# The experts' second product in matmuls of 256 columns instead of 512

## The chip, the cores and the metric

The kernel runs on one core of one Trainium2 chip. The metric is the device time of one execution in microseconds (us). Three runs of the kernel before took 2106.46, 2108.26 and 2109.92 us; their median, 2108.26 us, is the time before.

## The reference

A feature attention makes x (2304 tokens, 512 features), a gated product with three matrices makes a new x from it, and eight experts work on that. What the change touches is the last part:

```python
def _moe2_ref(x, w_gate, w1, w2):
    ...
    out = np.zeros((N, D), dtype=np.float32)
    for e in range(E):
        h = np.maximum(x @ w1[e], 0.0)
        ye = h @ w2[e]
        out += P[:, e:e + 1] * ye
    return out.astype(np.float32)
```

Here N = 2304 tokens, D = 512, E = 8 experts, and h has 1024 columns. P is made from x @ w_gate by an exponential and eight rounds of row and column scaling (the Sinkhorn steps).

## The kernel before

Three parts follow each other: the attention (to some 230 us), the gated product (to some 575 us), and the experts. All large products are made from operands that are split in two, a high part of type fp32r and a low part, so one product of tiles is three matmuls (`mm3`, lines 86 to 89): high times high, high times low, low times high. The first operand is the stationary one and is loaded before each matmul; the second is streamed, and its columns are the columns of the matmul.

The experts run in three token stages (`s`) of 768 tokens. In each stage the loop over `units` goes through experts `e` and, within an expert, through four units `p` (`NP` = 4). A unit (lines 724 to 752) makes seven products of 384 columns, 42 matmuls, into tiles `pa` and `ps` of PSUM; VectorE adds them up in `c` (line 741), and `h_split` (lines 720 to 722) makes two h tiles from that: ScalarE's ReLU gives `hH[p]` and `hH[p + 4]`, and VectorE then gives the low parts `hL[p]` and `hL[p + 4]`. So the last unit of an expert makes hH3, hL3, hH7 and hL7. In the first token stage ScalarE, VectorE and GpSimd also split the experts' weights (`prep_w1`, `split_w2`), and at a stage's last expert they split the x of the next stage (`prep_x`).

After an expert's fourth unit comes the second product, `h @ w2[e]`: for six blocks of 128 tokens (`tt`) one bank of PSUM, `py` (128 partitions x 512 columns, two buffers), is filled by eight h tiles in the order 0, 4, 1, 5, 2, 6, 3, 7 (`fts`), three matmuls of 512 columns each:

```python
for n, ft in enumerate(fts):
    hi, lo = W2[ft // 2]
    mm3(ps, hH[ft][:, tcs], hL[ft][:, tcs], hi[:, ft % 2], lo[:, ft % 2], n == 0, n == FT2 - 1)
    if n % 2:
        between()
```

That is 24 matmuls in a bank, 144 for an expert, and 3456 in the program. `between()` calls the next Sinkhorn step as long as there are any (the first expert of the first stage); their matmuls are at line 785 (`cs`). A full bank is read once by VectorE (line 847 or 849), which scales it by P and adds it to `o`.

The order of the instructions on each engine is made when the program is built, by a scheduler that may move an instruction of a later block ahead of one that waits. On the chip each engine goes through its own order, and waits on semaphores of the others.

Another place that the text speaks of is line 165 in the first part: fp32 matmuls of 128 columns, each on 64 of the 128 rows of the array, one for each half (`b`) side by side. The trace has two records for each of them.

Of the kernel before, what the change touches and what calls it, by code (L numbers as in the profile page):

```python
# [27 lines left out]
def kernel(  # L28
# [21 lines left out]
    NT, DM = out.shape  # L50
# [12 lines left out]
    FT2 = DF2 // P  # L63
# [22 lines left out]
    def mm3(ps, aH, aL, bH, bL, start, stop):  # L86
        nc.tensor.matmul(ps, aH, bH, start=start, stop=False)  # L87
        nc.tensor.matmul(ps, aH, bL, start=False, stop=False)  # L88
        nc.tensor.matmul(ps, aL, bH, start=False, stop=stop)  # L89
# [360 lines left out]
    def load_x(s):  # L450
        rawX[s] = rx.tile([P, KT, 2 * N1], F32, name=f"rx{s}", tag="rx")
        nc.sync.dma_start(rawX[s], XS[s])
# [29 lines left out]
    def load_w1(u):  # L482
        if u < len(units):
            s, e, p = units[u]
            if s > 0:
                return
            rawW1[u] = rw1.tile([P, 7, 2 * P], F32, name=f"r1_{u}", tag="r")
            nc.sync.dma_start(rawW1[u][:, 0:3], moe2_w1[e, p][:, 1:4])
            nc.sync.dma_start(rawW1[u][:, 3:7], W1T[u])

    def prep_w1(u):
        if u >= len(units):
            return
        n = u % len(W1S)
        if u >= len(W1S):
            pool = wc1c[0] if u % 3 == 2 else wc1
            hl = pool.tile([P, 2, 7, 2 * P], F32R, name=f"w1_{u}", tag="hl")
            nc.sync.dma_start(f32(hl), W1S[n])
            WC[u] = hl[:, 0], hl[:, 1]
            return  # L500
        r = rawW1.pop(u)
        hl = wc1.tile([P, 2, 7, 2 * P], F32R, name=f"w1_{u}", tag="hl")
        hi, lo = hl[:, 0], hl[:, 1]
        for i, c in enumerate((slice(0, 3), slice(3, 7))):
            copy("Wh", hi[:, c], r[:, c], 2 * u + i)
            subtract("Wl", lo[:, c], r[:, c], f32(hi[:, c]), 2 * u + i)
        nc.sync.dma_start(W1S[n], f32(hl))
        WC[u] = hi, lo

    def sbuf(c, name, bufs=1, side="right"):  # L510
        return c.enter_context(tc.tile_pool(name=name, bufs=bufs, side=side, reuse_waits="tile"))
# [30 lines left out]
    with ExitStack() as c2:  # L542
# [76 lines left out]
        for j in range(NT // N1):  # L619
            c0 = j * N1  # L620
            for ft in range(FT):
                ab = []
                for w in range(2):
                    n = 2 * ft + w
# [7 lines left out]
                    ps = ab_p.tile([P, N1], F32, name=f"ab{j}_{ft}_{w}", tag="ab")  # L632
                    hi, lo = w12[n]
# [25 lines left out]
            for dt in range(KT):  # L659
                ps = px_p.tile([P, N1], F32, name=f"px{j}_{dt}", tag="px")  # L660
                dc = slice(dt * P, (dt + 1) * P)
                for ft in range(FT):
                    hi, lo = w34[ft]
# [25 lines left out]
    with c4:  # L689
# [8 lines left out]
        W2, rawW2 = {}, {}  # L698
        hH = [hp.tile([P, 2 * N1], F32R, name=f"hH{i}") for i in range(FT2)]
        hL = [hp.tile([P, 2 * N1], F32R, name=f"hL{i}") for i in range(FT2)]  # L700

        def load_w2(u):
            if u < len(units):
                s, e, p = units[u]
                t = st.tile([P, 2, DM], F32, name=f"r2_{u}", tag="r")
                nc.sync.dma_start(
                    t, moe2_w2[e, 2 * p * P : 2 * (p + 1) * P, :].rearrange("(j p) d -> p j d", p=P)
                )
                rawW2[u] = t

        def split_w2(u):
            s, e, p = units[u]
            t = rawW2.pop(u)
            hi = wp.tile([P, 2, DM], F32R, name=f"w2h{u}", tag=f"h{p}")
            lo = wp.tile([P, 2, DM], F32R, name=f"w2l{u}", tag=f"l{p}")
            copy("W2h", hi, t, u)
            subtract("W2l", lo, t, f32(hi), u)
            W2[p] = hi, lo
# [5 lines left out]
        def unit(u, between):  # L724
            s, e, p = units[u]
            c = ut.tile([P, 4, N1], F32, name=f"c{u}", tag="c")
            c11, c21, c12, c22 = (c[:, i] for i in range(4))
            B11, B21, B22, T1, T2, T3, T4 = range(7)

            def product(x, i, *adds):  # L730
                ps = ph_p.tile([P, N1], F32, name=f"p{x}{u}", tag="ph")
                (wh, wl), (xh, xl) = WC[u], XC[x]
                for kt in range(2):
                    k = slice(kt * P, (kt + 1) * P)
                    mm3(ps, wh[:, i, k], wl[:, i, k], xh[:, kt], xl[:, kt], kt == 0, kt == 1)
                with tc.high_priority(60):
                    for o, t in adds:
                        if t is None:
                            nc.scalar.copy(o, ps)
                        else:  # L740
                            nc.vector.tensor_tensor(o, t, ps, ALU.add)  # L741
                between()

            product("a11", B11, (c11, None))
            product("s2", T2, (c12, c11))
            product("s3", T3, (c21, c12))
            product("s1", T1, (c22, c21), (c12, c12))
            product("a12", B21, (c11, c11))
            product("a22", T4, (c21, c21))
            h_split(p, c[:, 0:2].rearrange("p a n -> p (a n)"))  # L750
            product("s4", B22, (c12, c12))
            h_split(p + NP, c[:, 2:4].rearrange("p a n -> p (a n)"))
# [47 lines left out]
        def between():  # L800
            if todo:
                todo.pop()()
# [3 lines left out]
        for u, (s, e, p) in enumerate(units):  # L806

            if u + 1 < len(W1S):
                prep_w1(u + 1)
                load_w1(u + 2)  # L810
            if u + 2 == len(W1S):
                c6.close()
                wc1c.append(sbuf(c6, "wc1c", 1, "left"))
            if u + 2 >= len(W1S):
                prep_w1(u + 2)
            unit(u, between)
            split_w2(u)
            load_w2(u + 2)
            if p < NP - 1:
                continue  # L820
            if e == 0 and s + 1 < NSC:
                load_x(s + 1)
            if e == NE - 1 and s + 1 < NSC:
                prep_x(s + 1)
            for tt in range(2 * N1 // P):
                t = s * 2 * N1 // P + tt
                ps = py_p.tile([P, DM], F32, name=f"py{e}_{t}", tag="py")
                tcs = slice(tt * P, (tt + 1) * P)
                if e == 0:
                    oacc[tt] = op.tile([P, DM], F32, name=f"o{t}", tag=f"o{tt}")  # L830
                o = oacc[tt]
                fts = [f for p_ in range(NP) for f in (p_, p_ + NP)]
                for n, ft in enumerate(fts):
                    hi, lo = W2[ft // 2]
                    mm3(ps, hH[ft][:, tcs], hL[ft][:, tcs], hi[:, ft % 2], lo[:, ft % 2], n == 0, n == FT2 - 1)
                    if n % 2:
                        between()
                if todo:
                    pend.append(t)
                    nc.scalar.copy(o, ps)  # L840
                    continue
                for t_ in pend:
                    o_ = oacc[t_]
                    nc.vector.tensor_scalar(o_, o_, Pw[:, t_, 0:1], None, ALU.mult)
                pend = []
                if e == 0:
                    nc.vector.tensor_scalar(o, ps, Pw[:, t, 0:1], None, ALU.mult)  # L847
                else:
                    nc.vector.scalar_tensor_tensor(o, ps, Pw[:, t, e : e + 1], o, ALU.mult, ALU.add)  # L849
                if e == NE - 1:  # L850
                    nc.sync.dma_start(out[t * P : (t + 1) * P, :], o)
# [76 lines left out]
```

## Time and profile before

| | us |
|---|---|
| median of 3 runs (lowest, highest) | 2108.26 (2106.46, 2109.92) |
| the profiled execution | 2110.07 |
| its span, first to last instruction | 2108.3 |
| TensorE (PE) busy in the span | 2050.1 |
| weight loads (PEld) | 1817.4 |
| VectorE (DVE) | 1129.7 |
| ScalarE (ACT) | 597.6 |
| GpSimd (POOL) | 363.0 |

The profile is of one execution. Busy time of an engine is the time in which at least one of its instructions is under way; TensorE's weight loads have a row of their own, since they run beside its matmuls. Matmuls overlap each other, and their ends are modelled, so the rate of TensorE is read from the starts. The releaser of an idle stretch is the instruction that ended the wait. The granted clock is the share of TensorE's full clock in a stretch.

### The profile page before, as it was taken

To read this page: it belongs to the slowest core of one execution; us is meant where nothing else is said; L and a number is where in the kernel's file an instruction comes from. 1 tells how busy PE (TensorE), PEld (TensorE's weight loads), DVE (VectorE), ACT (ScalarE), POOL (GpSimd) and SP (SyncE) were. 2 spreads that over 40 slices of the span, in tenths; PEclk is the share of its full clock that TensorE was granted. 3 is DMA by queue.
4 is the path that set the end of the run, shared out by engine and by line. 5 is a ranking of instruction groups with operands and counts; after the bars stand their busy time and mean duration, and the time that the engine had idled before them with its cause. 6 is when DMAs were issued, how large, how long until landed. Compare 5 with 4: busy or idle time off the path is not lost.

```text
span 2108.3 us, 28910 instructions
## 1 busy us (share of the span) xinstructions
PE 2050.1 (97%) x11877; PEld 1817.4 (86%) x11877; DVE 1129.7 (54%) x1718; ACT 597.6 (28%) x979; POOL 363.0 (17%) x268
## 2 busy tenths in 40 slices
PE   7999899999899999999999999999999999999999
PEld 5667689999788888888888999888999888999887
DVE  7765853333486545665454555434565444555443
ACT  6765532222333222333221222111132111122111
POOL 3433331211322211222220000000010000000000
PEclk9999999999899999999999999999999999999999
DMA  6432445555565555655564444334454334444330
GB/s 216 144 118 84 137 134 155 185 155 155 198 247 182 192 196 220 249 198 192 185 230 150 180 180 149 134 107 151 179 190 179 131 107 153 170 180 174 124 117 30
DMA packets 78531, 345.44 MB, mean 164 GB/s; under 512 B 7488, under 2 KB 11456, under 8 KB 65728
## 3 DMA queue, kind: packets, MB, share of 16 engines
q1 hardware_dynamic: 77808, 342.95, 45.6%
q8 instruction: 93, 1.52, 0.3%
q10 hardware_dynamic: 592, 0.66, 0.1%
q14 instruction: 38, 0.31, 0.0%
HBM read 256.54 MB, written 87.03 MB: 163 GB/s over the span
## 4 chain that ended last, share of the span: by engine, by line
PE 82%; DVE 6%; ACT 3%; DMA 3%; issue 3%; POOL 3%; SPq 0%; ACTq 0%; POOLq 0%; DVEq 0%
PE py L89 13%; PE py L88 12%; PE py L87 12%; PE ps L87 5%; PE ps L89 5%; PE ps L88 5%; PE pa L87 4%; PE pa L89 4%; PE pa L88 4%; PE ab L89 3%; PE ab L87 3%; PE ab L88 3%; PE px L88 1%; PE px L89 1%; PE px L87 1%
## 5 line engine op out<-in xcount | busy, mean ns | idle before, releaser
L89 PE MATMUL py<-w2h,hL 128*128 128x512 f32 x1152 | 457.1, 397 | 0.2
L87 PE MATMUL py<-w2h,hH 128*128 128x512 f32 x1152 | 456.8, 397 | 0.4 <-DVE o L847 0.4
L88 PE MATMUL py<-w2l,hH 128*128 128x512 f32 x1152 | 456.9, 397 | 0.0
L849 DVE SCALAR_TENSOR_TENSOR o<-py,Pw,o 128x512 f32<-128x512 f32 x126 | 94.6, 750 | 451.5 <-PE py L89 451.4
L99 POOL TENSOR_TENSOR w2l<-r,w2h 128x1024 fp32r<-128x1024 f32 x48 | 116.4, 2424 | 1109.2 <-ACT w2h L96 1100.2
L741 DVE TENSOR_TENSOR c<-c,ps 128x384 f32<-128x384 f32 x480 | 255.7, 548 | 88.8 <-PE ps L89 83.1
L96 ACT CAST w2h<-r 128x1024 fp32r<-128x1024 f32 x96 | 101.0, 1052 | 695.2 <-PE py L89 612.7
L89 PEld LDWEIGHTS py<-w2h,hL 128*128 128x128 f32 x1152 | 216.8, 188 | 55.3 <-DVE hL L722 3.0
L87 PEld LDWEIGHTS py<-w2h,hH 128*128 128x128 f32 x1152 | 217.0, 188 | 52.5 <-DVE o L847 0.8
L88 PEld LDWEIGHTS py<-w2l,hH 128*128 128x128 f32 x1152 | 217.0, 188 | 51.5
L722 DVE SCALAR_TENSOR_TENSOR hL<-c,hH 128x768 fp32r<-128x768 f32 x192 | 233.0, 1230 | 28.0 <-ACT hH L721 26.4
L721 ACT ACTIVATE hH<-c 128x768 fp32r<-128x768 f32 x192 | 158.0, 843 | 298.7 <-DVE c L741 276.7
L87 PE MATMUL ab<-XH,wH 128*128 128x384 f32 x384 | 131.2, 342 | 8.6 <-DVE wH L96 8.6
L89 PE MATMUL ab<-XH,wL 128*128 128x384 f32 x384 | 131.6, 343 | 1.1 <-DVE wL L99 1.1
L88 PE MATMUL ab<-XL,wH 128*128 128x384 f32 x384 | 130.9, 341 | 0.0
L741 DVE TENSOR_TENSOR c<-c,pa 128x384 f32<-128x384 f32 x192 | 102.2, 548 | 16.7 <-PE pa L89 15.2
L643 POOL TENSOR_TENSOR cL<-a,cH 128x384 fp32r<-128x384 f32 x48 | 58.8, 1227 | 235.1 <-ACT cH L642 235.0
L99 POOL TENSOR_TENSOR w<-r,w 128x768 fp32r<-128x768 f32 x32 | 66.6, 2081 | 129.6 <-ACT w L96 124.8
L99 DVE TENSOR_TENSOR w2l<-r,w2h 128x1024 fp32r<-128x1024 f32 x48 | 59.0, 1229 | 54.7 <-ACT w2h L96 54.7
L96 ACT CAST w<-r 128x768 fp32r<-128x768 f32 x64 | 59.6, 938 | 97.8 <-DMA r<-in_moe_w_dram 31.0
L641 DVE TENSOR_TENSOR a<-ab,a 128x384 f32<-128x384 f32 x48 | 26.7, 556 | 108.6 <-PE ab L89 108.6
L87 PEld LDWEIGHTS ab<-XH,wH 128*128 128x128 f32 x384 | 72.9, 190 | 10.4 <-DVE wH L96 8.3
(174 smaller groups left out, 3840.8 us busy)
## 6 DMA issues: line engine op xcount, KB each, us to landing
w<-w1s SPq DMA_DIRECT2D x64, 1792.0 KB, 7.6
w1s<-w SPq DMA_DIRECT2D x32, 1792.0 KB, 6.6
r<-in_moe_w_dram SPq DMA_DIRECT2D x96, 512.0 KB, 3.5
rw<-in_w_dram SPq DMA_DIRECT2D x32, 512.0 KB, 3.8
tr<-in_moe_w_dram SPq DMA_DIRECT2D x32, 512.0 KB, 4.3
w1t<-tt SPq DMA_DIRECT2D x32, 512.0 KB, 5.1
r<-w1t SPq DMA_DIRECT2D x32, 512.0 KB, 8.1
r<-in_moe_w_dram SPq DMA_DIRECT2D x32, 384.0 KB, 7.5
```

Of the source, the lines that this page charges most:

```text
L87: nc.tensor.matmul(ps, aH, bH, start=start, stop=False)
L88: nc.tensor.matmul(ps, aH, bL, start=False, stop=False)
L89: nc.tensor.matmul(ps, aL, bH, start=False, stop=stop)
L96: (e.copy if e is nc.scalar else e.tensor_copy)(out, src)
L99: engine(key, i).tensor_tensor(out, a, b, ALU.subtract)
L641: behind = nc.vector.tensor_tensor(cc, ab[1], a_sb, ALU.mult).ins
L643: nc.gpsimd.tensor_tensor(l, cc, f32(h), ALU.subtract)
L721: nc.scalar.activation(hH[ft], src, AF.Relu)
L722: nc.vector.scalar_tensor_tensor(hL[ft], src, 0.0, f32(hH[ft]), ALU.max, ALU.subtract)
L741: nc.vector.tensor_tensor(o, t, ps, ALU.add)
L849: nc.vector.scalar_tensor_tensor(o, ps, Pw[:, t, e : e + 1], o, ALU.mult, ALU.add)
```

## The change

Each bank is filled in two halves (`hf`) of 256 columns, one after the other. For each half all eight h tiles are gone through, so every h tile is the stationary operand twice as often. The bank, the instruction that reads it and the number of calls of `between()` in a bank (four) are the same.

```diff
-                for n, ft in enumerate(fts):
-                    hi, lo = W2[ft // 2]
-                    mm3(ps, hH[ft][:, tcs], hL[ft][:, tcs], hi[:, ft % 2], lo[:, ft % 2], n == 0, n == FT2 - 1)
-                    if n % 2:
-                        between()
+                for hf in range(2):
+                    dc = slice(hf * DM // 2, (hf + 1) * DM // 2)
+                    for n, ft in enumerate(fts):
+                        hi, lo = W2[ft // 2]
+                        mm3(
+                            ps[:, dc], hH[ft][:, tcs], hL[ft][:, tcs],
+                            hi[:, ft % 2, dc], lo[:, ft % 2, dc], n == 0, n == FT2 - 1,
+                        )
+                        if n % 4 == 3:
+                            between()
```

All 3456 matmuls of `py` with 512 columns become 6912 with 256. On TensorE, the end of the first pass through the h tiles in the first bank of expert 2, first token stage, stood so before (`py2_0` is the bank of expert 2, block 0; the last operand is the stationary one):

```order
L87 MATMUL py2_0_7238<-w2h11_7232,hH6_5846 128x512
L88 MATMUL py2_0_7238<-w2l11_7233,hH6_5846 128x512
L89 MATMUL py2_0_7238<-w2h11_7232,hL6_5854 128x512
L87 MATMUL py2_0_7238<-w2h9_7078,hH3_5843 128x512
L88 MATMUL py2_0_7238<-w2l9_7079,hH3_5843 128x512
L89 MATMUL py2_0_7238<-w2h9_7078,hL3_5851 128x512
L87 MATMUL py2_0_7238<-w2h11_7232,hH7_5847 128x512
L88 MATMUL py2_0_7238<-w2l11_7233,hH7_5847 128x512
L89 MATMUL py2_0_7238<-w2h11_7232,hL7_5855 128x512
```

The last of these is matmul 24 of the bank, with 23 ahead of it. In the changed kernel the same place, in the first half of the bank, reads:

```order
L87 MATMUL py2_0_7526<-w2h9_7366,hH3_5843 128x256
L88 MATMUL py2_0_7526<-w2l9_7367,hH3_5843 128x256
L89 MATMUL py2_0_7526<-w2h9_7366,hL3_5851 128x256
L87 MATMUL py2_0_7526<-w2h11_7520,hH7_5847 128x256
L88 MATMUL py2_0_7526<-w2l11_7521,hH7_5847 128x256
L87 MATMUL py2_1_7576<-w2h8_7289,hH0_5840 128x256
L88 MATMUL py2_1_7576<-w2l8_7290,hH0_5840 128x256
L89 MATMUL py2_1_7576<-w2h8_7289,hL0_5848 128x256
L87 MATMUL py2_1_7576<-w2h10_7443,hH4_5844 128x256
L89 MATMUL py2_0_7526<-w2h11_7520,hL7_5855 128x256
L87 MATMUL py2_0_7526<-w2h8_7289,hH0_5840 128x256
```

Four matmuls of the next bank (`py2_1`) have moved ahead of the one with hL7, which has 27 matmuls ahead of it now; the second half of the bank follows. It is so for experts 2 to 6 of this stage; for expert 1 there are 30 ahead, for expert 7 there are 34, and for expert 7 of the second stage 35. At the 15 other experts after the first no matmul is moved, and 23 are ahead.

On ScalarE, at the last unit of expert 2 in the first stage (unit 11, whose sums are in `c11`; `w1` is the weight of later units), the order before was:

```order
L739 COPY c11_7170<-pa1111_7171 128x384
L721 ACTIVATE hH6_5846<-c10_7093 128x768
L96 CAST w1_12_7161<-r1_12_7090 128x1024
L96 CAST w1_13_7394<-r1_13_7167 128x768
L721 ACTIVATE hH3_5843<-c11_7170 128x768
L721 ACTIVATE hH7_5847<-c11_7170 128x768
L96 CAST w1_13_7394<-r1_13_7167 128x1024
```

and is now:

```order
L739 COPY c11_7458<-pa1111_7459 128x384
L721 ACTIVATE hH6_5846<-c10_7381 128x768
L96 CAST w1_12_7449<-r1_12_7378 128x1024
L721 ACTIVATE hH3_5843<-c11_7458 128x768
L721 ACTIVATE hH7_5847<-c11_7458 128x768
L96 CAST w1_13_7826<-r1_13_7455 128x768
L96 CAST w1_13_7826<-r1_13_7455 128x1024
```

The cast of `w1_13` with 768 columns has moved from before hH3 to behind hH7. VectorE's order at these places is as before.

## Rows read from the trace of the kernel before

**Rows 1.** The page: busy time of each engine, and the chain by engine.
```profile
PE 2050.1 (97%) x11877; PEld 1817.4 (86%) x11877; DVE 1129.7 (54%) x1718; ACT 597.6 (28%) x979; POOL 363.0 (17%) x268
...
PE 82%; DVE 6%; ACT 3%; DMA 3%; issue 3%; POOL 3%; SPq 0%; ACTq 0%; POOLq 0%; DVEq 0%
```

**Rows 2.** The page's costliest groups: busy us, mean ns of one, idle before.
```profile
L88 PE MATMUL py<-w2l,hH 128*128 128x512 f32 x1152 | 456.9, 397 | 0.0
...
L88 PEld LDWEIGHTS py<-w2l,hH 128*128 128x128 f32 x1152 | 217.0, 188 | 51.5
```

**Rows 3.** Window of second stage: us, busy PE, PEld, DVE, ACT, POOL (count), clock, DMA.
```profile
1127.00:1614.00 487.00, 487.00 (x2405) 434.03 (x2405) 234.76 (x338) 99.52 (x129) 42.76 (x18) 1.00 0.40 148
```

**Rows 4.** Timeline of TensorE, expert 1 of second stage: start us, us, instruction.
```profile
1190.06 0.39 PE L87 MATMUL py<-w2h,hH 128*128 128x512 f32 x1
...
1223.79 0.34 PE L87 MATMUL pa<-a11h,w 128*128 128x384 f32 x1
...
1252.94 0.39 PE L87 MATMUL py<-w2h,hH 128*128 128x512 f32 x1
```

**Rows 5.** Timeline at the start of a second product: matmuls and a load.
```profile
1000.83 0.40 PE L88 MATMUL py<-w2l,hH 128*128 128x512 f32 x1
1000.83 0.19 PEld L89 LDWEIGHTS py<-w2h,hL 128*128 128x128 f32 x1
...
1001.06 0.39 PE L89 MATMUL py<-w2h,hL 128*128 128x512 f32 x1
```

**Rows 6.** Timeline of lines 605 and 606 (six matmuls), and their loads' group.
```profile
300.50 0.34 PE L605 MATMUL lg<-XH,WG 128*16 128x384 f32 x1
...
301.37 0.34 PE L606 MATMUL lg<-XL,WG 128*16 128x384 f32 x1
...
L606 PEld LDWEIGHTS lg<-XL,WG 128*16 128x16 f32 x24 | 2.3, 94 | 5.0 <-DVE XL L671 3.7
```

**Rows 7.** Timeline of line 165, and tile pp: ns min/median/max of its records.
```profile
103.31 0.72 PE L165 MATMUL pp<-wpr,k 64*128 64x128 f32 x9
...
L165 PEld LDWEIGHTS pp<-wpr,k x288: 182/188/330, 3.5 to 216.6; 64*128 64x128 f32 x144
L165 PE MATMUL pp<-wpr,k x288: 272/272/578, 3.5 to 216.7; 64*128 64x128 f32 x144
```

**Rows 8.** Timeline of line 785, and tile cs: ns of its loads and matmuls.
```profile
587.87 0.41 PE L785 MATMUL cs<-Pw,ones 128*128 128x144 f32 x2
...
L785 PEld LDWEIGHTS cs<-Pw,ones x16: 186/188/338, 587.8 to 637.3; 128*128 128x128 f32 x16
L785 PE MATMUL cs<-Pw,ones x16: 283/288/577, 587.9 to 637.4; 128*128 128x144 f32 x16
```

**Rows 9.** Timeline where second products begin: latest, earliest of eight, one of fifteen.
```profile
745.08 0.39 PE L87 MATMUL py<-w2h,hH 128*128 128x512 f32 x1
...
746.39 0.84 ACT L96 CAST w<-r 128x768 fp32r<-128x768 f32 x1 [4.43 <-DMA r<-in_moe_w_dram]
...
748.01 2.83 DVE L722 SCALAR_TENSOR_TENSOR hL<-c,hH 128x768 fp32r<-128x768 f32 x2 [0.84 <-ACT hH L721]
...
1000.60 0.39 PE L87 MATMUL py<-w2h,hH 128*128 128x512 f32 x1
...
1002.97 2.41 DVE L722 SCALAR_TENSOR_TENSOR hL<-c,hH 128x768 fp32r<-128x768 f32 x2 [0.45 <-ACT hH L721]
...
1190.73 1.95 DVE L722 SCALAR_TENSOR_TENSOR hL<-c,hH 128x768 fp32r<-128x768 f32 x2
```

**Rows 10.** Windows of TensorE after two waits: us, busy (count), clock, DMA, GB/s.
```profile
595.40:597.40 2.00, 0.34 (x2) 1.00 0.55 229
597.50:601.50 4.00, 4.00 (x24) 1.00 0.98 328
606.90:608.90 2.00, 0.47 (x3) 0.92 0.56 237
608.60:612.00 3.40, 3.10 (x10) 0.50 0.97 405
```

## The prediction

> **What bounds the kernel now.** I read the page's busy shares and chain first: TensorE is busy 97% of the span and carries 82% of the chain that ended last [rows 1]. So the time is, nearly everywhere, the number of matmuls times the distance from one matmul's start to the next one's. The recorded length of a matmul (397 ns, [rows 2]) is not that distance: matmuls overlap in the pipeline. The windows by stage come second: between 1127 and 1614 us TensorE has no idle time at all, at a granted clock of 1.00, which is its 2.4 GHz level [rows 3]. Third, the timeline gives the distances. From the first matmul of an expert's second product at 1190.06 to the first matmul after it at 1223.79 there are 144 matmuls of 512 columns: 33.73 us / 144 = 234.2 ns each. From there to 1252.94 there are 168 matmuls of 384 columns: 29.15 / 168 = 173.5 ns each [rows 4]. Nothing else is on the path there, so a change of the distance at the second product is paid or gained in full. That product has 3 x 1152 = 3456 matmuls (its three lines have the same count, [rows 2]): 3456 x 234.2 ns = 809 us of the span.
>
> Each matmul loads its own weights (one load record per matmul, 188 ns, [rows 2]). The load of the next starts with the matmul before it: load 1000.83, matmul before it 1000.83, its own matmul 1001.06 [rows 5]. Today a load of 188 ns lies wholly beside a 234 ns distance.
>
> **The change, part by part.** It replaces 3456 matmuls of 512 columns by 6912 of 256, and so adds 3456 matmuls and 3456 weight loads. The orders show that all of them really have 256 columns, and that no other instruction count changes; each bank is still read once, by one instruction on VectorE, and the fillers are still called four times per bank.
>
> *Term 1, the distance at 256 columns, p.* No row has this shape, so I bound it. Upper end: a 256-column matmul will hardly take longer than a 384-column one, 173.5 ns. Lower end: the fp32 matmuls of the first stage (line 165). Their record of 272 ns is the nearest to what a 256-column one should show (397 ns at 512 columns, about 340 at 384, so about 280), and each has a load of 188 ns like the ones here. They run in two halves of the array side by side: nine of them cover 0.72 us, so the ninth starts 0.72 - 0.27 = 0.45 us after the first, four steps of one half: 112 ns per step (111.5 where I need the digit) [rows 7]. A 188 ns load thus does not force a 188 ns distance: most of its record overlaps the next one. Nearest for a load of the whole array are the two matmuls of line 785: they cover 0.41 us with a record of 288, so they start 0.12 us apart, with 188 ns loads [rows 8]. So the load alone should bind no later than 112 to 122 ns. Between these I choose by the two known sizes. A line through 384 and 512 columns has a slope of (234.2 - 173.5) / 128 = 0.474 ns a column and leads to 173.5 - 128 x 0.474 = 112.8 at 256. A plain proportion from 512 gives 117.1. That 384 columns cost 173.5 is no effect of loading: with loads of 16 columns (94 ns) the distance is (301.37 - 300.50) / 5 = 174 too [rows 6]. I take **112.8**, since the nearest row, 111.5, lies on that side. Two halves then cost 225.6 instead of 234.2: 8.6 ns x 3456 = **-29.7 us**. The ends: p = 111.5 gives -38.7, p = 117.1 gives 0, p = 122 gives +34.
>
> Here a rule speaks against the change. The row shows the load starting with the matmul before it on the same full array, and the distance staying at 234 [rows 5]. The Trainium skill (TensorE: Matmul & The Clock Gate, Part 3, "The mechanism") says that a weight load overlaps with matmuls in flight only when the row group differs, which here it never does. By that the added loads would stand in the open, hundreds of microseconds; the trace does not agree. The same page ("Back-to-back issue gap") gives N/2.4 + 2.5 ns for a warm matmul. By it two halves cost 218.3 instead of 215.8, so the term would be an estimated +8.6 us; the rows are 234.2 and 173.5 where it has 215.8 and 162.5, so the trace does not agree on the size of what comes on top of the columns.
>
> *Term 2, the wait for the last unit's hL.* Within a bank the matmuls go through the h tiles in order, and the last two pairs (hH3, hL3, hH7, hL7) are made while the first bank already runs. Before, the first matmul with hL7 was number 24 of the bank, 23 x 234 ns = 5.4 us after its start. Now it comes at half the pace; the order of PE puts four matmuls of the next bank ahead of it and no more, so it is due 27 x 112.8 = 3.05 us after the start. Ready it is at 750.84 for a bank begun at 745.08, 5.76 us, the latest of eight such boundaries, and at 1005.38 for one begun at 1000.60, 4.78 us, the earliest of the eight [rows 9]. These eight are experts 1 to 7 of the first token stage, where VectorE also splits weights, and the last expert of the second, where it splits x. In the order, five of the eight have 27 matmuls ahead, the others 30, 34 and 35, 29.25 on average: 3.30 us. With the middle of the two ends, 5.27: (5.27 - 3.30) x 8 = **+15.8 us**. On ScalarE one cast moves from before hH3 to behind hH7 in experts 2 to 6; it delayed hH3 only where its data came late, as at 746.39 [rows 9], so I leave it at nothing, its cover being VectorE's own backlog; if it helps, it gives back a few tenths at some boundaries. At the 15 other boundaries hL7 is ready 2.62 us after the start (1190.73 + 1.95 against 1190.06, [rows 9, 4]) and due after 23 x 112.8 = 2.59: +0.03 x 15 = **+0.4 us**. This cover is gone to the last few hundredths; a p of 117 would restore it (2.69).
>
> *Term 3, the clock after those waits.* Rows show that an idle stretch of about 2 us may cost more than itself: after the one around 596 us the clock stayed at 1.00, after the one around 608 it was 0.50, the 1.2 GHz level, for 3.4 us [rows 10]. At half clock 3.4 us lose 1.7. I take two of the eight waits to do so: **+3.4 us**; ends 0 and 8 x 1.7 = 13.6.
>
> *At nothing:* the fetching of 6912 more instructions (matmuls and loads), which does not make TensorE wait today, as it has no idle time in [rows 3]; without that cover TensorE would show waits with "issue" as releaser. The Sinkhorn steps of the first expert, whose matmuls move among the smaller pieces: some microseconds either way, no more than the one wait before 608.9 us [rows 10] could bring or take. The end of the program: the last bank is read by the same instruction.
>
> *Sum:* -29.7 + 15.8 + 0.4 + 3.4 = -10.1 us. Against the profiled execution's own 2110.07 us (span 2108.3 and 1.8 around it) that is 2100.0. That execution lies 1.8 above the median of the runs shown, so I predict **2098**, faster by 0.5%. A measurement can tell about 0.2% here, 4.2 us, from no change.
>
> **The rivals.**
> 1. *Proportional columns (slower).* p = 117.1: the stream gains nothing, and the waits decide alone: 8 x (5.27 - 29.25 x 0.1171) = 14.8, with the clock 3.4: +18, 2126. It decides from the p at which term 1 falls below terms 2 and 3: 19.6 / 3456 = 5.7 ns per pair, p = 114.3. For it: 173.5 / 384 and 234.2 / 512 are nearly the same per column. Against: the smaller size is the cheaper one per column, and line 165 steps at 111.5.
> 2. *A fixed cost per matmul (slower).* If a column took one period of 2.4 GHz, 384 columns would be 160 ns and 13.5 would be left per matmul; paid twice, p = 120.2, +21 from the stream, some 13 + 3 from the waits: 2146. Against: 512 columns leave 20.9, so it is not fixed.
> 3. *The load binds (slower).* At p = 122, the upper estimate from line 785, +34 + 16: 2158; if 188 ns bound, +490. Against: line 165. That the load does not overlap at all costs up to 188 x 3456 = 650 us, near 2760; [rows 5] exclude it almost wholly. The rule of the Trainium skill on row groups, above, is this case.
> 4. *Gain and waits cancel.* p between 113.7 and 114.9: within 4.2 us of before, 2108.
> 5. *The waits shrink.* VectorE keeps its order at these boundaries, but part of its lateness is ScalarE's; with half of term 2 and p = 111.5 to 112.8: 2080 to 2090.
>
> That the change does not do what it says is excluded by the orders.
>
> **How the numbers follow.** Forecast (p from 111.5 to 113.7, rival 5 in it) 0.45; cancelling 0.20; proportional 0.22; fixed cost 0.07; load 0.05; no overlap 0.01. So faster 0.45, same 0.20, slower 0.35. The likeliest case alone holds 2080 to 2104. The range goes from 2080 (p = 111.5 with halved waits) to 2136 (proportional, with most of the clock's 13.6) and leaves out rivals 2 and 3 and a little on either side.
>
> **What would show it.** Two halves in a 48-matmul bank from 1127 us on: 5.41 us per bank instead of 5.62, and 63 us per expert become 61.6; load records still starting with the matmul before. In the first stage, at each expert's first bank, a wait of TensorE on VectorE's hL, about 2 us, seven times, and one near 1570. Clock 0.50 behind a few of them. Wrong would be: a distance above 115 ns (rivals 1 to 3, told apart by whether it is 117, 120 or more), or waits much shorter than 2 us.

## The result, and the profile after

The changed kernel is **slower by 1.4%**: 2138.68 us, the median of 4 runs (2134.81 to 2144.88), beside 2108.24 of the kernel before (4 runs); the ratio is 1.0145, with an interval of 1.013 to 1.016. The prediction, 2098 and faster, had the wrong sign, and the time lies outside its range.

The page of the changed kernel, at the places of [rows 1, 2]:

```profile
PE 2070.1 (97%) x15333; PEld 1994.2 (93%) x15333; DVE 1119.3 (52%) x1718; ACT 596.2 (28%) x979; POOL 363.0 (17%) x268
...
L89 PE MATMUL py<-w2h,hL 128*128 128x256 f32 x2304 | 649.5, 282 | 6.3 <-DVE hL L722 6.3
L87 PE MATMUL py<-w2h,hH 128*128 128x256 f32 x2304 | 648.3, 282 | 2.9 <-ACT hH L721 2.6
```

The 3456 matmuls more are there, and TensorE is as busy as before; but two new rows of idle time stand at the second product, behind hL and behind hH. The span is 2138.8 us, 30.5 more than before. The distance of two starts is read as in [rows 4], from the timeline of TensorE. Here are the first matmul of a second product and the first one after it, for two experts of the second stage and one of the third:

```profile
1210.89 0.28 PE L87 MATMUL py<-w2h,hH 128*128 128x256 f32 x1
...
1245.13 0.34 PE L87 MATMUL pa<-a11h,w 128*128 128x384 f32 x1
...
1274.25 0.28 PE L87 MATMUL py<-w2h,hH 128*128 128x256 f32 x1
...
1308.13 0.34 PE L87 MATMUL pa<-a11h,w 128*128 128x384 f32 x1
...
1654.33 0.28 PE L87 MATMUL py<-w2h,hH 128*128 128x256 f32 x1
...
1688.92 0.34 PE L87 MATMUL pa<-a11h,w 128*128 128x384 f32 x1
```

The 288 matmuls took 34.24, 33.88 and 34.59 us, where 144 of 512 columns took 33.73. With a stop of 0.06 us behind hL7 taken off, that is 118.65, 117.42 and 119.88 ns from start to start. Every expert after the first has one of these three levels; the mean is 118.9. Two halves cost 237.7 instead of 234.2, not the forecast 225.6. The loads still start with the matmul before them:

```profile
1211.25 0.28 PE L87 MATMUL py<-w2h,hH 128*128 128x256 f32 x1
1211.25 0.19 PEld L88 LDWEIGHTS py<-w2l,hH 128*128 128x128 f32 x1
```

In the first token stage TensorE now stops at each boundary. Expert 4, beginning at 883.89, is the clearest; TensorE, then VectorE, then ScalarE:

```profile
883.89 0.28 PE L87 MATMUL py<-w2h,hH 128*128 128x256 f32 x1
...
887.40 0.38 PE L87 MATMUL py<-w2h,hH 128*128 128x256 f32 x1 [1.21 <-ACT hH L721]
...
888.39 0.38 PE L89 MATMUL py<-w2h,hL 128*128 128x256 f32 x1 [0.49 <-DVE hL L722]
...
883.40 1.21 DVE L99 TENSOR_TENSOR w<-r,w 128x1024 fp32r<-128x1024 f32 x1
884.53 1.01 DVE L741 TENSOR_TENSOR c<-c,ps 128x384 f32<-128x384 f32 x2
885.46 1.01 DVE L741 TENSOR_TENSOR c<-c,pa 128x384 f32<-128x384 f32 x2
886.39 0.54 DVE L741 TENSOR_TENSOR c<-c,ps 128x384 f32<-128x384 f32 x1
887.38 1.83 DVE L722 SCALAR_TENSOR_TENSOR hL<-c,hH 128x768 fp32r<-128x768 f32 x2 [0.44 <-ACT hH L721]
...
886.50 1.58 ACT L721 ACTIVATE hH<-c 128x768 fp32r<-128x768 f32 x2 [4.78 <-DVE c L741]
```

TensorE waits for hH3 and for hL3. hL7 comes at 887.38 + 1.83 = 889.21, and nothing waits for it here. When the second product begins, VectorE still has a weight split of 1.21 us and five additions of the last unit ahead of it; ScalarE had waited 4.78 us for them. The clock did not fall behind these stops, as a window behind the wait and one of the first stage show (columns as in [rows 3]); in the later two stages it is 1.00 as well.

```profile
888.60:892.00 3.40, 3.40 (x30) 3.40 (x30) 0.61 (x1) 0.21 (x1) 2.03 (x1) 1.00 0.95 294
...
584.00:1147.00 563.00, 545.33 (x3825) 536.45 (x3824) 327.04 (x498) 162.05 (x208) 115.46 (x52) 1.00 0.57 206
```

So the 30.5 us of the span come from these places (read from the starts of matmuls, before and after):

| | us |
|---|---|
| the parts ahead of the experts, whose code is the same (576.3, 580.2) | +3.9 |
| first expert of the first stage (105.2, 105.1), and what follows the last matmul (4.4, 4.2) | -0.3 |
| distances in the second products, 23 experts | +11.7 |
| waits for hH3, hL3 and hL7 there (10.9 in stage 1, where before had 1.6; 1.2 at the second stage's last expert; 0.06 at 15 others) | +11.4 |
| products of experts 2 to 7 of the first stage (178.7, 182.5) | +3.8 |

I take the first row as scatter: in the other kernels of this study, whose code there is the same, that part took 575.3 to 579.4 us. The last row was in no term. (The expectations below number these products by the second product ahead of them, 1 to 6.) It is the third unit of an expert, where a product waits for VectorE's addition to empty a bank: the group of line 87 for `ps<-s2h`, experts 2 to 7, in the kernel before and in the changed one.

```profile
L87 PE MATMUL ps<-s2h,w 128*128 128x384 f32 x48 | 16.5, 344 | 2.2 <-DVE c L741 2.1
```

```profile
L87 PE MATMUL ps<-s2h,w 128*128 128x384 f32 x48 | 16.5, 344 | 5.0 <-DVE c L741 5.0
```

### The profile page after: what moved, and what is told of

It is laid out like the page before. It is cut to its first block, busy times and chain, and to the rows that moved or that the text cites. A ratio compares the mean times of both kernels' runs of the same rounds, so it can differ in the third digit from the quotient of the medians.

```text
span 2138.8 us, 35819 instructions
## 1 busy us (share of the span) xinstructions
PE 2070.1 (97%) x15333; PEld 1994.2 (93%) x15333; DVE 1119.3 (52%) x1718; ACT 596.2 (28%) x979; POOL 363.0 (17%) x268
## 4 chain that ended last, share of the span: by engine, by line
PE 79%; DVE 7%; issue 4%; ACT 4%; DMA 3%; POOL 2%; SPq 0%; DVEq 0%; ACTq 0%; POOLq 0%
PE py L89 13%; PE py L88 12%; PE py L87 12%; PE ps L87 5%; PE ps L89 5%; PE ps L88 5%; PE pa L87 4%; PE pa L89 4%; PE pa L88 4%; PE ab L89 3%; PE ab L87 3%; PE ab L88 3%; DVE c L741 2%; DMA r<-in_moe_w_dram 2%; PE px L89 1%
## 5 line engine op out<-in xcount | busy, mean ns | idle before, releaser
L89 PE MATMUL py<-w2h,hL 128*128 128x256 f32 x2304 | 649.5, 282 | 6.3 <-DVE hL L722 6.3
L87 PE MATMUL py<-w2h,hH 128*128 128x256 f32 x2304 | 648.3, 282 | 2.9 <-ACT hH L721 2.6
L88 PE MATMUL py<-w2l,hH 128*128 128x256 f32 x2304 | 647.1, 281 | 0.0
L89 PEld LDWEIGHTS py<-w2h,hL 128*128 128x128 f32 x2304 | 436.0, 189 | 8.5 <-DVE hL L722 8.3
L87 PEld LDWEIGHTS py<-w2h,hH 128*128 128x128 f32 x2304 | 436.4, 189 | 4.3 <-ACT hH L721 4.1
L88 PEld LDWEIGHTS py<-w2l,hH 128*128 128x128 f32 x2304 | 436.1, 189 | 0.0
L99 POOL TENSOR_TENSOR w2l<-r,w2h 128x1024 fp32r<-128x1024 f32 x48 | 117.1, 2439 | 1121.1 <-ACT w2h L96 1105.8
L722 DVE SCALAR_TENSOR_TENSOR hL<-c,hH 128x768 fp32r<-128x768 f32 x192 | 227.5, 1203 | 48.7 <-ACT hH L721 47.5
L99 POOL TENSOR_TENSOR w<-r,w 128x768 fp32r<-128x768 f32 x32 | 67.1, 2098 | 142.9 <-ACT w L96 129.3
```

The lines of the kernel that those rows point to most:

```text
L99: engine(key, i).tensor_tensor(out, a, b, ALU.subtract)
L722: nc.vector.scalar_tensor_tensor(hL[ft], src, 0.0, f32(hH[ft]), ALU.max, ALU.subtract)
```

## The experiments

**Theory after the result:** the 256 columns cost their proportion (117.1 ns), the nearness to the load of 128 columns adds up to 3 ns, and the waits come from halving the first bank of an expert. **Rivals:** a fixed cost in each matmul; a load that alone sets the distance; waits that have other causes than the pace of the first bank.

### Where the waits are: the first bank whole, or only the first bank halved

```diff
-                for hf in range(2):
-                    dc = slice(hf * DM // 2, (hf + 1) * DM // 2)
+                cuts = (0, DM) if tt == 0 else (0, DM // 2, DM)
+                step = 2 * (len(cuts) - 1)
+                for c0, c1 in zip(cuts, cuts[1:]):
+                    dc = slice(c0, c1)
...
```

> Only the first bank of each expert is filled with matmuls of 512 columns as before; the other five are filled in halves. Theory (the cost has two parts of about equal size: the distance of 256-column matmuls of about 119 ns, and the waits for the last unit's hL in the first bank): the waits go, 5/6 of the stream's part stays, 5/6 x (6912 x 119 - 3456 x 234.2) = about +11 us over before, 2119. Rival 'waits alone': as before, 2108. Rival 'matmuls alone': 5/6 of the 30 us stay, 2133.

It took 2116.36 us, ratio 1.0038 (1.0024 to 1.0052). The waits for hL are gone from the second products of experts 2 to 5 (33.78 us each; 34.2 to 34.3 at experts 1, 6 and 7). In the second stage an expert reads:

```profile
1259.15 0.39 PE L87 MATMUL py<-w2h,hH 128*128 128x512 f32 x1
...
1264.76 0.28 PE L87 MATMUL py<-w2h,hH 128*128 128x256 f32 x1
...
1292.92 0.34 PE L87 MATMUL pa<-a11h,w 128*128 128x384 f32 x1
...
1322.05 0.39 PE L87 MATMUL py<-w2h,hH 128*128 128x512 f32 x1
```

The five halved banks are 240 matmuls in 28.16 us, 117.3 ns each, and the expert has 62.90 us where it had 62.89. Twice as many matmuls of half the length, with no wait in them, gain nothing and lose nothing here. What is left over before is the first expert (+2.0) and the products of experts 2 to 7 (+3.75).

The counterpart halves the first bank alone, `cuts = (0, DM // 2, DM) if tt == 0 else (0, DM)`.

> Only the first bank of each expert is filled in halves, the other five with 512 columns. Theory: the waits stay, 1/6 of the stream's part stays: +2 from the stream and +12 to +16 from waits in and behind the first bank, 2122 to 2126. Rival 'waits alone': 2135 to 2138. Rival 'matmuls alone': +5, 2113.

It took 2134.28 us, ratio 1.0118 (1.0103 to 1.0133): with a sixth of the new matmuls, most of the loss. Experts 1 to 7 of the first stage took 459.39 us, 13.8 more than before, and stages two and three only 1.9 and 0.7 more. The time was above what was expected, by the first expert: its order changed, and it took 112.2 us instead of 105.2. So the waits belong to the first bank, as term 2 had it.

### The same halves without the early need

Here both halves of a bank are made side by side, h tile by h tile. The last unit's tiles are then due as late as before.

```diff
-                for hf in range(2):
-                    dc = slice(hf * DM // 2, (hf + 1) * DM // 2)
-                    for n, ft in enumerate(fts):
-                        hi, lo = W2[ft // 2]
+                for n, ft in enumerate(fts):
+                    hi, lo = W2[ft // 2]
+                    for hf in range(2):
+                        dc = slice(hf * DM // 2, (hf + 1) * DM // 2)
...
```

> The two halves of a bank are not filled one after the other but side by side: each h tile is used for the left and then for the right 256 columns before the next h tile. The same 6912 matmuls of 256 columns and as many loads, but the h tiles are needed at the old pace. Theory: no waits for hL, the stream's part whole: about +13, 2121. Rival 'waits alone': 2108. Rival 'matmuls alone': 2138.

2128.51 us, ratio 1.0094 (1.0079 to 1.0109), some 7 above the expectation, again by the first expert (113.6 us, +8.4). The distance is 118.66 ns in all of the second stage, with no stop at all. So the second and third stage lose 3.2 and 3.3 us by the distance alone, and the first, with 1.8 us of waits left, 3.2. Lines 87 and 88 have the same stationary operand one after the other, here as in the other kernels; it is loaded for each of them (6912 load records for 6912 matmuls), and the second comes no sooner.

### What sets the distance: other sizes

In this kernel the six banks of an expert are cut as 128+384, 192+320, 224+288, 256+256, 160+352 and 512.

```diff
+                cuts = ((0, 128, 512), (0, 192, 512), (0, 224, 512), (0, 256, 512), (0, 160, 512), (0, 512))[tt]
+                step = 2 * (len(cuts) - 1)
+                for c0, c1 in zip(cuts, cuts[1:]):
+                    dc = slice(c0, c1)
...
```

> The six banks of each expert are cut at different places: 128+384, 192+320, 224+288, 256+256, 160+352 columns and 512 whole. What is read is the distance between matmuls by their columns. 'Columns set it, proportionally': 58, 73, 88, 102, 117, 132, 146, 161 and 174 ns at 128, 160, 192, 224, 256, 288, 320, 352 and 384 columns. 'The load sets a floor': the same above some 260 columns, and a floor between 110 and 120 ns for all of 224 columns and fewer; then 256 columns lie at the edge of the floor.

The third expert of the second stage (24 matmuls from row to row, 48 of 256):

```profile
1332.39 0.25 PE L87 MATMUL py<-w2h,hH 128*128 128x192 f32 x1
...
1335.05 0.33 PE L87 MATMUL py<-w2h,hH 128*128 128x320 f32 x1
...
1338.59 0.27 PE L87 MATMUL py<-w2h,hH 128*128 128x224 f32 x1
...
1341.27 0.30 PE L87 MATMUL py<-w2h,hH 128*128 128x288 f32 x1
...
1344.48 0.28 PE L87 MATMUL py<-w2h,hH 128*128 128x256 f32 x1
...
1350.11 0.23 PE L87 MATMUL py<-w2h,hH 128*128 128x160 f32 x1
...
1352.75 0.36 PE L87 MATMUL py<-w2h,hH 128*128 128x352 f32 x1
```

| columns | 160 | 192 | 224 | 256 | 288 | 320 |
|---|---|---|---|---|---|---|
| ns from start to start | 110 | 111 | 112 | 117.3 | 134 | 148 |
| ns a column | 0.69 | 0.58 | 0.50 | 0.458 | 0.464 | 0.461 |

Above 256 columns the distance is nearly proportional, and below it there is a floor of 110 to 112 ns that hardly depends on the columns. Of these sizes 256 is the smallest above the floor. A fixed cost in each matmul is not excluded by this: rival 2 asks for 133.5 ns at 288 columns and 146.8 at 320, as near to the table as the proportion; the next run decides. The whole took 2230.67 us (one run); the short pieces pay the floor, and the early ones leave hL less time still.

### Whose floor it is: loads of 64 columns

With the same cuts, two of three matmuls now have a stationary operand of 64 columns; they make only half of the tokens, so half of the two correction products is left out. The third keeps its 128.

```diff
+                half = slice(tt * P, tt * P + P // 2)
...
+                        nc.tensor.matmul(ps[:, dc], hH[ft][:, tcs], hi[:, ft % 2, dc], ...)
+                        nc.tensor.matmul(top, hH[ft][:, half], lo[:, ft % 2, dc], ...)
+                        nc.tensor.matmul(top, hL[ft][:, half], hi[:, ft % 2, dc], ...)
```

> The same cuts as in the run with six sizes, but the matmuls of high times low and of low times high use only the first 64 tokens of a block as their stationary operand, so their loads have 64 columns instead of 128 (the other 64 tokens lack these two terms). Theory (the floor of 111 to 112 ns seen at 128 to 224 columns is the load of 128 columns): before a matmul with the short load the distance falls below the floor, towards the proportional 58, 73, 88 and 102 ns at 128, 160, 192 and 224 columns, and stays near 111 before the full load. Rival (a matmul has a floor of its own): 111 to 112 everywhere.

At 192 columns, matmuls and loads (the loads in a fence behind):

```profile
1321.95 0.27 PE L841 MATMUL py<-w2h,hH 128*128 128x192 f32 x1
1322.06 0.25 PE L842 MATMUL py<-w2l,hH 128*64 128x192 f32 x1
1322.15 0.25 PE L843 MATMUL py<-w2h,hL 128*64 128x192 f32 x1
1322.23 0.27 PE L841 MATMUL py<-w2h,hH 128*128 128x192 f32 x1
```

```profile
1321.86 0.19 PEld L841 LDWEIGHTS py<-w2h,hH 128*128 128x128 f32 x1
1321.97 0.14 PEld L842 LDWEIGHTS py<-w2l,hH 128*64 128x64 f32 x1
1322.06 0.14 PEld L843 LDWEIGHTS py<-w2h,hL 128*64 128x64 f32 x1
1322.15 0.19 PEld L841 LDWEIGHTS py<-w2h,hH 128*128 128x128 f32 x1
```

From a load of 128 columns to the next load it is 0.11 us; from a load of 64 columns to the next, 0.09, and 192 x 0.458 = 88 ns is what the columns ask for. So the floor is the load of 128 columns, and where it is short the columns set the distance. The whole took 2202.09 us (one run). I had put the short distance ahead of the matmul with the short load; the records show it behind. Unrounded, a load of 128 columns holds the next one up by 108 to 109 ns. The Trainium skill (TensorE: Matmul & The Clock Gate, Part 2, "LDWEIGHTS (loading the stationary operand)") gives P / 1.2 ns for P columns, an estimated 107 at 128; at the 0.458 ns a column of this run a matmul needs an estimated 233 columns to cover that, and the trace agrees: 224 columns lie on the floor, 256 above it.

Behind a matmul with the short load the mean distance is 74, 88 and 103 ns at 160, 192 and 224 columns, and 231 at 512: 0.45 to 0.46 ns a column. With the fixed cost of rival 2 it would be 80, 93.5 and 107 at the first three. That excludes it.

The same loads with all banks in halves of 256 (the changed kernel with those three matmuls):

> All banks in two halves of 256 columns as in the changed kernel, with the same short loads of 64 columns for two of three matmuls (the second 64 tokens of each block lack two terms). Theory (at 256 columns the columns need 116 to 117 ns, and the nearness of the load's floor adds up to 3): before the short loads the distance is 115 to 117 in every expert, before full loads 117 to 120, and the levels of 118.7 and 119.9 ns by expert go or shrink. Rival (the columns alone set 117 to 120): no difference between short and full loads, levels as before.

```profile
1207.79 0.28 PE L839 MATMUL py<-w2h,hH 128*128 128x256 f32 x1
...
1241.15 0.34 PE L87 MATMUL pa<-a11h,w 128*128 128x384 f32 x1
```

It took 2127.81 us (one run). This expert's 288 matmuls took 33.36 us, with one stop of 0.04: 115.7 ns each, which is 0.452 ns a column, as at 384 ([rows 4], 173.5 / 384). In the later two stages every other expert has that, and those between have 117.75. With full loads it is 117.4 to 119.9. So two shorter loads of three bring the distance down by some 2 ns, but levels remain, and the ranges overlap: in the run with six sizes 256 columns took 117.9 ns, with the same short loads. The proportion of 0.45 to 0.46 covers 115 to 118 ns. What is above it fits a load of 108 to 109 ns that adds up to 3 ns from close by, though it is the shorter of the two; that it is the cause is not shown.

### Where the three levels come from

Here the third bank stays whole, `cuts = (0, DM) if tt == 2 else (0, DM // 2, DM)`.

> As the changed kernel, but the third bank of each expert is filled with matmuls of 512 columns. What is read is the mean distance of 256-column matmuls ahead of that bank and behind it. Theory (the level of 117.3, 118.7 or 119.9 ns is a matter of how the run of matmuls started, and is taken over from one bank to the next): levels as in the changed kernel ahead of it, 117.3 behind it in all experts, as where the first bank was whole. Rival (the level belongs to the expert, by its addresses or its data): the same level ahead and behind.

It took 2134.68 us (one run). The level changes across the whole bank inside one expert: 117.3 ns ahead of it and 118.7 behind in the expert that begins at 1209.58 us, 118.7 and 117.3 in that at 1335.96, 119.9 and 118.7 in that at 1588.42. So it belongs neither to an expert nor to its data. It is not always 117.3 behind, as I had expected. The traces show where it is set, too: in the changed kernel each of these experts begins at 118.4 to 118.5 ns and has its level from the stop in its first bank on, be it one of 0.06 us. With the halves side by side, experts without a stop stay at 118.7 to their end, and those with one have 117.3 to 117.5 behind it. So a restart sets it, behind a stop or a bank of 512 columns; what about the restart chooses among the levels, the runs don't show.

### What makes hL late

The 1024-column half of each weight split goes from VectorE to GpSimd, in the changed kernel, the kernel before, and the one with the first bank whole:

```diff
-    Xl="v", Xs="g", Wt="v", Wh="a", Wl="gv", W2h="a", W2l="vg",
+    Xl="v", Xs="g", Wt="v", Wh="a", Wl="g", W2h="a", W2l="vg",
```

> The changed kernel with the low half of every weight split of 1024 columns made on GpSimd instead of VectorE (line 99; 1.2 us on VectorE, once per unit). Theory: the waits for hL in the first token stage come from VectorE being behind. At 884 us, when the second product of an expert begins, VectorE has still five of the last unit's additions to make, and one such split of 1.21 us stands right ahead of them. Then hL3 and hL7 come about 1.2 us earlier at each of the seven boundaries, and the waits in the second products of the first stage fall from 10.9 us to about 3 or 4: 2131 to 2133 us. The waits of the products for VectorE's additions (1.17 us an expert) should fall as well, by at most 3.9 in all: 2128 at best. Rival: the lateness starts on ScalarE, whose cast waits 4 us for its DMA and holds up hH behind it; then the waits stay at 9 to 11 us and the time within 2 us of 2138.7. Second rival: GpSimd's split is twice as slow and slows VectorE beside it (hL takes 1.96 us instead of 0.95 where they run together), so the waits grow: over 2141.

2157.37 us, ratio 1.0229 (1.0214 to 1.0244). Two opposite things happened. The products' wait is nearly gone: in the same six experts the group of line 87 has no idle time (0.9 us stands at `pa<-a11h` instead), and the products took 178.9 us, as before the change (178.7).

```profile
L87 PE MATMUL ps<-s2h,w 128*128 128x384 f32 x48 | 16.5, 345 | 0.0
```

So VectorE's split is needed for this wait. It isn't where the lateness begins, though. In the changed kernel, in the units of expert 4, ScalarE, VectorE and TensorE read:

```profile
860.75 1.05 ACT L96 CAST w2h<-r 128x1024 fp32r<-128x1024 f32 x1 [1.41 <-DMA r<-in_moe_w_dram]
...
863.31 1.78 DVE L722 SCALAR_TENSOR_TENSOR hL<-c,hH 128x768 fp32r<-128x768 f32 x1 [1.69 <-ACT hH L721]
...
870.29 0.41 PE L87 MATMUL ps<-s2h,w 128*128 128x384 f32 x1 [0.84 <-DVE c L741]
```

ScalarE's cast waits for its DMA, the hH behind it is late, and VectorE stands idle for it. In the kernel before VectorE's idle time at this place was 0.37, 0.21, 1.00, 0.19, 0.57 and 0.13 us in experts 2 to 7, and TensorE's wait 7 to 8 us later 0.36, 0.21, 0.84, 0.17, 0.56 and 0.11. So the lateness goes through VectorE almost whole. With the split on GpSimd the hH is as late (8.8 to 9.9 us after the second product's end), but VectorE makes most of it up in time. In the changed kernel it starts 8.9 to 9.0 us after that end (before: 7.3 to 8.2); a cast of 0.83 us that stood behind it stands ahead of it now, and the cast shown is mostly later too.

But the stops in the second products became longer, by the second rival: those of experts 1 to 7 took 270.2 us, 250.1 without the edit. In expert 4, where the bank begins at 899.64:

```profile
901.35 0.55 DVE L741 TENSOR_TENSOR c<-c,ps 128x384 f32<-128x384 f32 x1
902.34 0.96 DVE L722 SCALAR_TENSOR_TENSOR hL<-c,hH 128x768 fp32r<-128x768 f32 x1 [0.45 <-ACT hH L721]
903.81 1.98 DVE L722 SCALAR_TENSOR_TENSOR hL<-c,hH 128x768 fp32r<-128x768 f32 x1 [0.51 <-ACT hH L721]
...
905.85 0.44 PE L89 MATMUL py<-w2h,hL 128*128 128x256 f32 x1 [1.28 <-DVE hL L722]
906.09 0.41 PE L87 MATMUL py<-w2h,hH 128*128 128x256 f32 x1
906.30 0.41 PE L88 MATMUL py<-w2l,hH 128*128 128x256 f32 x1
```

The window behind that stop:

```profile
906.00:908.00 2.00, 2.00 (x10) 2.00 (x11) 0.00 (x0) 0.00 (x0) 0.00 (x0) 0.51 0.81 251
```

The last addition ends 901.90 - 899.64 = 2.3 us after the start, instead of 886.93 - 883.89 = 3.0. But a cast stands on ScalarE between hH3 and hH7 now, and hL7 takes 1.98 us with GpSimd's split beside it, where hL3 just before took 0.96. It is ready after 6.2 us instead of 5.3. Behind the stops the clock falls to 0.51, the 1.2 GHz level, and matmuls of 256 columns start 0.21 us apart (906.09, 906.30). The first expert, in a new order, cost 9.4 us more than in the changed kernel.

> The kernel before with the same splits on GpSimd. It has waits of 1.6 us in its second products and of 4.1 us in the products of experts 1 to 6 of the first stage. Theory of VectorE's backlog: most of these go, 2104 to 2106. Rival (ScalarE and its DMA): within 2 us of 2108.3. GpSimd's slower split as a new bound: over 2111.

> The first bank of each expert in matmuls of 512 columns, the others in halves, as in the run with the first bank whole (2116.4 us, no waits for hL), and the same splits on GpSimd. Its first stage still has 7 us of the products' waits for VectorE in experts 1 to 6. Theory of VectorE's backlog: 3 to 5 us of them go, about 2112. Rival: 2116 as before. If a second product in halves is only as good as one in 512 columns, it doesn't come below 2108.

2114.50 us (ratio 1.003, 1.002 to 1.0041) and 2119.03 (1.0049, 1.0034 to 1.0064): both slower than without the edit, and both by the first expert (113.1 and 112.8 us, against 105.2 and 107.2). Outside of it the kernel before gains 1 us at most: its products of experts 2 to 7 fall from 178.7 to 176.0, its second products of stage 1 rise by 1.7. No kernel of this study beats the one before.

The last one leaves the work where it is and puts hH and hL ahead of the weight splits in the scheduler's order:

```diff
         def h_split(ft, src):
-            nc.scalar.activation(hH[ft], src, AF.Relu)
-            nc.vector.scalar_tensor_tensor(hL[ft], src, 0.0, f32(hH[ft]), ALU.max, ALU.subtract)
+            with tc.high_priority(60):
+                nc.scalar.activation(hH[ft], src, AF.Relu)
+                nc.vector.scalar_tensor_tensor(hL[ft], src, 0.0, f32(hH[ft]), ALU.max, ALU.subtract)
```

> The changed kernel with the two instructions of h_split, hH on ScalarE and hL on VectorE, put ahead of the weight splits in the scheduler's order. On VectorE hL of the first three units moves ahead of one addition and of the split behind it; hL3 and hL7 stand behind the same work as before. On ScalarE a cast of 768 columns stands ahead of hH3 again, as in the kernel before. If VectorE's backlog (the sum of the work ahead of hL7) sets the waits, the time stays within 3 us of 2138.7, outside the first expert, whose order changes and may bring or take some microseconds. If the places of hH and hL in the order set it, the waits of the products (7 us in experts 1 to 6) and of the second products (10.9) fall by half: about 2130.

2138.57 us, 0.1 from the changed kernel. The stops of stage 1 stay (11.3 us, 10.9 without the edit), and the products of experts 2 to 7 take 185.3 us instead of 182.5, with their waits at other places. With the cast back ahead of hH3, hL7 is ready after 4.8 to 5.4 us at experts 2, 3, 5 and 6, instead of 4.2 to 4.4 (at expert 4 after 5.0 instead of 5.3). So this order brings nothing; it doesn't tell the work ahead of hL from ScalarE's waits for its DMA. The run also shows that the levels are no matter of the order: from 1147.2 us on, where TensorE, VectorE and ScalarE have the same order in both, its two stages took 985.7 us, the changed kernel's 991.6. Expert 0 of the third stage, from its second product to that of the next:

```profile
1653.56 0.28 PE L87 MATMUL py<-w2h,hH 128*128 128x256 f32 x1
...
1716.56 0.28 PE L87 MATMUL py<-w2h,hH 128*128 128x256 f32 x1
```

63.00 us with 117.4 ns, where the changed kernel had 63.73 with 119.9. It may be why its four runs lie 10 us apart, and those of the kernel before, beside it, 3.5 (6.1 in a later set of eleven); that is not shown.

## Why the prediction was wrong

- **What bounds the kernel** held: TensorE's distances and its stops account for all but the scatter of the early part.
- **Term 1 failed**, and with it the sign: +11.7 us instead of -29.7. The step that failed is the line through 384 and 512 columns. I read the 0.0056 ns a column by which 512 is dearer (234.2 / 512 against 173.5 / 384) as a slope of 0.474 with a negative start, and carried it down to 112.8. The runs show nearly a proportion instead, 0.452 to 0.468 from 256 columns up: 117.4 to 119.9 ns at 256, 118.9 in the mean. The 112 ns of line 165 [rows 7], which I took as a sign for the low value, fit the floor by the load: 128 columns at 0.452 ns would be 58. They bound the distance from below and say nothing of what 256 columns cost.
- **The load** was not left out, but taken as a bound that decides only beyond 112 to 122 ns. In the runs it is a floor of 108 to 112, and 256 columns lie above it. So rival 1 (the proportion, 117.1) holds in the main, and some 2 ns are left that the proportion doesn't give; a part of rival 3 may be in them, but the cause stays open. Rival 2 gave nearly the measured distance, 120.2, for a reason that the short loads exclude. The Trainium skill's rule that a load overlaps only where the row group differs (TensorE: Matmul & The Clock Gate, Part 3, "The mechanism"), which I had set aside by [rows 5], is against the trace here too: loads start with the matmul before them, on the whole array, 119 ns apart. What the Trainium skill says elsewhere on the same page (Part 2, "Back-to-back issue gap"), that both the load and the matmul set the spacing, is what the runs show.
- **Term 2** was right in its mechanism and its place, and too large. At the eight boundaries TensorE stopped for 12.1 us in all; before had 1.6 of them already, so the change added 10.5, where 15.8 were forecast. It waits for hH3 and hL3 where I had computed hL7; and hL7 was ready earlier than before (4.41 instead of 5.77 us at expert 2), with the cast moved behind hH7, which I had put at nothing or a few tenths. At the 15 others 0.06 us each came, 0.9 instead of 0.4.
- **Term 3** was nothing: the clock stayed at 1.00. Its mechanism exists: with GpSimd's split, behind four stops of 2.3 us in all in one bank (1.7 in two in expert 4 here), it fell to 0.51.
- **Put at nothing:** fetching the added instructions cost nothing visible in the expert stages. The products' wait, +3.8, was in no term: in an expert's third unit TensorE waits for VectorE, which has been late since ScalarE's cast waited for its DMA, some 9 us earlier. That the wait goes with VectorE's split was tried; that the DMA and the moved cast make it longer than before is read from the traces alone.
- By [rows 10] I allowed the first expert some microseconds either way; in the changed kernel it was 0; in ten of the eleven experiments it was +1 to +11.5, in the other -0.8.

## What to carry to other kernels

Where every matmul loads its own stationary operand, halving the columns can gain only what the long form wastes over a proportion (here under 3 ns of 234), and it brings the distance down to the load's own time, where it begins to lose. Measure a size, or a third one, before a line through two is carried to it. And look at what is made just in time: half the pace in an early pass halves the cover of the operands that come last.

## What the runs showed of the hardware

- A load of 128 columns holds the next load up by 108 to 109 ns, though its record has 188; one of 64 columns by 61 to 63 at most (the medians behind it at 128 columns, in the run with six sizes and short loads).
- At 256 columns, close above that, the distance takes one of three constant levels (117.4, 118.65, 119.9 ns), set anew at a stop, even one of 0.06 us, and different between two kernels with the same order of instructions there.
- With a second split on GpSimd for each unit, the same hL instruction on VectorE took longer: its median of 56 in the first stage's last seven experts rose from 958 to 1636 ns, its mean from 1317 to 1502.
